# Attention ahead of a mixture of experts: work moved between VectorE, GpSimd and ScalarE, products of several query chunks in one PSUM bank, row maxima in half tiles

## The chip, the core and the metric

The kernel runs on one core of one Trainium2 chip. Its time is the device time of one execution in microseconds (us); the median of the runs is what counts. Engines: TensorE (PE, matmuls into PSUM), VectorE (DVE), ScalarE (ACT, activations), GpSimd (POOL) and SyncE (SP, which issues the DMAs here).

## What is computed

```python
q_pool = q.reshape(B, H, S // 2, 2, D).mean(axis=3)          # B, H, S, D = 4, 8, 1152, 64
scores = scale * np.matmul(q_pool, k.transpose(0, 1, 3, 2))
scores = scores - np.max(scores, axis=-1, keepdims=True)
attn = np.exp(scores)
attn = attn / (np.sum(attn, axis=-1, keepdims=True) + 1e-09)
x = np.matmul(attn, v)
```

The result x (2304 rows of 512) goes through a mixture of experts in which each of eight experts takes exactly 288 rows, picked by the largest logits (h = relu(x w1), y = h w2), and then through a feed-forward layer with g = h cos(h) between its two products. The products need more than half precision, so operands are held as a high and a low half in float16 and multiplied in three products, hi*hi, hi*lo and lo*hi.

## The kernel before

Attention is worked off in 16 units. A unit is one head of two batches, called sides 0 and 1; side 0 has queries 0 to 511 and a rest of 64, side 1 a rest of 64 and 512 more, so that a unit has nine chunks of 128 queries, of which chunk 4 holds the two rests. The keys of a side are nine blocks of 128.

For every unit:

- The operands are loaded and split (`prep_q` L342, `prep_k` L384, `prep_v` L422, the last two once for each side). `upper` (L327) writes the high half on ScalarE or GpSimd, a scalar_tensor_tensor on VectorE the low half (L372, L404, L440); DMA transposes turn q and k.
- `row_max` (L487) multiplies a chunk of queries with eight blocks of keys into a pair of PSUM banks s (two pairs in turn), and one VectorE reduction of 1024 columns (L496) takes the maximum; `last_max` (L467) does the ninth block for four chunks at a time, in banks t. `shift` (L500) joins the two maxima (L508) and writes them in two halves, 16 copies each, beside q (L511, L513), so that a matmul subtracts them from the scores.
- `piece` (L547): the scores of a unit are made with the keys on the partitions, in eleven pieces. Ten have 1024 columns in two PSUM banks t (three banks in turn), the eleventh 128. ScalarE takes exp of each bank into a float32 tile p (L565). Pieces 3 and 8 are used as they are, in float32. For the other nine ScalarE makes the high half ph (L597, one instruction of 1024 columns), and the low half pl = p - ph is divided between GpSimd (columns from d on, L607) and VectorE (columns below d, L614), with d chosen so that both would end together.
- `product` (L644): for each chunk of queries, ph and pl of all keys are multiplied with v and a column of ones into the one bank acc; `evac` (L669) adds the two parts of 65 columns on VectorE (L671).
- `finish` (L706): the sum is inverted (L713, L715), the result scaled (L339, on VectorE or GpSimd), for every second unit split into halves xs (L738 on ScalarE, L740 on VectorE), stored, turned, and multiplied with the gate weights into logits.

The order of the instructions on each engine is made when the kernel is built, by class `Order` (L72): tasks ask for an engine and a number of columns, a table COST counts the engines' time, and each task has a rank (ten to a unit). The engines then run their lists strictly in that order. Besides, `split64` (L189) splits pieces of the float64 weight w_in with what time is left: 23 of its 32 pieces come before the end of attention.

After attention, `moe` does the routing (a search by bits on VectorE and TensorE that begins with a maximum over the logits, L940), the experts and the last layer.

## Time and profile before

| | us |
|---|---|
| median of 3 runs | 1282.27 (1281.61 to 1290.19) |
| span of the profiled execution, first to last instruction | 1280.3 |
| busy in the span: PE / DVE / ACT / POOL | 1070.1 / 988.0 / 714.7 / 550.7 |
| attention: first scores to last | about 33 to 553 |

The page does not give a device time of its own for the profiled execution; the median lies 2.0 us above its span. Busy times are those in which an engine works on instructions, waits for data or a port inside an instruction included. The ends of matmuls are modelled.

### The profile page before, as it was taken

Reading aid. Unit: us, or ns where it says so; the run is one execution under the profiler, and the core shown is the slowest. Engines: PE = TensorE matmul, PEld = TensorE weight load, DVE = VectorE, ACT = ScalarE, POOL = GpSimd, SP = SyncE. Lnnn points to the kernel's source line nnn. Section 1 sums busy time; section 2 is a strip of 40 time slices with the busy share of each in tenths; the row PEclk is TensorE's granted clock in tenths of the full one; section 3 lists DMA queues with packets and bytes.
Section 4 is the critical chain, followed back from the end, with each engine's and each line's share of the span. In section 5 each row is a group of like instructions: output and inputs, shape, how many; then the busy total and the mean of one; then the engine's idle time right before and its main releaser. Section 6 shows DMA issues by size and latency. Waiting matters only on the chain. (4 is left out here: it accounts for less than half of the span.)

```text
span 1280.3 us, 26070 instructions
## 1 busy us (share of the span) xinstructions
PE 1070.1 (84%) x10281; PEld 729.8 (57%) x10281; DVE 988.0 (77%) x1927; ACT 714.7 (56%) x1324; POOL 550.7 (43%) x474
## 2 busy tenths in 40 slices
PE   3788877888788787851687999999999999999997
PEld 1355555555555555541464575766757576676763
DVE  7999999999999999779699686493847746271632
ACT  2766667677676767756577353362524436261533
POOL 1674667666666755547467112121120313030222
PEclk9999889999898989975798999999999999999999
DMA  6855655665566353234543262412223243300000
GB/s 183 208 117 140 150 124 131 141 136 139 129 128 121 81 121 63 51 96 142 153 139 100 77 170 70 117 44 77 68 101 86 75 112 85 74 29 17 1 17 17
DMA packets 195546, 128.93 MB, mean 101 GB/s; under 512 B 143008, under 2 KB 161440, under 8 KB 195424
## 3 DMA queue, kind: packets, MB, share of 16 engines
q1 hardware_dynamic: 192448, 117.83, 37.3%
q0 software_dynamic: 2976, 9.44, 2.2%
q8 instruction: 80, 1.31, 0.4%
q14 instruction: 42, 0.34, 0.1%
HBM read 83.40 MB, written 9.45 MB: 73 GB/s over the span
## 5 line engine op out<-in xcount | busy, mean ns | idle before, releaser
L607 POOL TENSOR_TENSOR pl<-p,ph 128x832 f16<-128x832 f32 (+6 forms) x128 | 222.9, 1745 | 98.2 <-ACT ph L597 74.5
L1294 POOL TENSOR_TENSOR gl<-turns,gh 128x512 f16<-128x512 f32 x72 | 89.0, 1243 | 306.8 <-ACT gh L1292 306.6
L565 ACT ACTIVATE p<-t 128x512 f32<-128x512 f32 x256 | 146.4, 593 | 103.2 <-PE t L578 84.0
L636 PE MATMUL acc<-vv,ph 128*128 128x130 f16 (+1 forms) x1124 | 129.2, 227 | 81.9 <-DVE o L671 80.1
L496 DVE TENSOR_REDUCE nm<-s 128x1 f32<-128x1024 f32 x144 | 173.9, 1211 | 1.7 <-PE s L453 1.5
L1309 PE MATMUL h<-yh,wih 128*128 128x256 f16 x576 | 158.5, 275 | 0.9 <-DVE turns L1287 0.9
L1309 PE MATMUL h<-yh,wil 128*128 128x256 f16 x576 | 157.8, 274 | 0.0
L1309 PE MATMUL h<-yl,wih 128*128 128x256 f16 x576 | 157.8, 274 | 0.0
L636 PEld LDWEIGHTS <-pl 128*128 128x128 f16 (+1 forms) x1152 | 97.1, 104 | 94.9 <-issue 88.9
L578 PE MATMUL t<-q,k 96*128 96x512 f16 (+1 forms) x576 | 143.5, 304 | 3.3 <-DMA q<-q 3.3
L577 PE MATMUL t<-q,k 128*128 128x512 f16 (+1 forms) x576 | 142.9, 304 | 3.0 <-ACT p L565 2.3
L597 ACT ACTIVATE ph<-p 128x1024 f16<-128x1024 f32 x128 | 134.8, 1054 | 1.3
L1204 DVE SCALAR_TENSOR_TENSOR hl<-h,hh 128x288 f16<-128x288 f32 x64 | 29.1, 454 | 121.2 <-ACT hh L1202 121.2
L636 PE MATMUL acc<-vv,pl 128*128 128x65 f16 (+1 forms) x1124 | 121.6, 197 | 0.4 <-DVE pl L614 0.4
L636 PEld LDWEIGHTS <-ph 128*128 128x128 f16 (+1 forms) x1152 | 107.2, 110 | 25.7 <-issue 15.3
L1309 PEld LDWEIGHTS <-wih 128*128 128x128 f16 x1152 | 108.4, 98 | 16.7 <-issue 1.2
L1335 PE MATMUL o<-woh,gl 128*128 128x512 f16 x288 | 110.3, 383 | 3.9 <-POOL gl L1294 3.9
L1335 PE MATMUL o<-wol,gh 128*128 128x512 f16 x288 | 110.3, 383 | 0.9 <-POOL wol L239 0.9
L1335 PE MATMUL o<-woh,gh 128*128 128x512 f16 x288 | 110.4, 383 | 0.1
L453 PE MATMUL s<-k,q 128*128 128x512 f16 (+1 forms) x320 | 93.9, 408 | 13.2 <-DVE nm L496 12.1
L1230 PE MATMUL h<-xx,w1h 128*128 128x288 f16 x512 | 97.5, 291 | 0.4 <-ACT xx L1116 0.4
L1335 PEld LDWEIGHTS <-gh 128*128 128x128 f16 x576 | 54.4, 98 | 66.7 <-issue 6.6
(267 smaller groups left out, 2623.9 us busy)
## 6 DMA issues: line engine op xcount, KB each, us to landing
wraw<-in_moe_w_dram SPq DMA_DIRECT2D x64, 512.0 KB, 5.0
kr<-in_k_dram SPq DMA_DIRECT2D x32, 288.0 KB, 3.1
vr<-in_v_dram SPq DMA_DIRECT2D x32, 288.0 KB, 3.0
qr<-in_q_dram SPq DMA_DIRECT2D x32, 256.0 KB, 3.5
raw<-in_moe_w_in_dram SPq DMA_DIRECT2D x32, 256.0 KB, 3.0
raw<-in_moe_w_out_dram SPq DMA_DIRECT2D x32, 256.0 KB, 3.0
k<-k SPq DMA_DIRECT2D x32, 144.0 KB, 2.8
x_dram<-xs SPq DMA_DIRECT2D x16, 160.0 KB, 2.6
```

Source lines behind the costliest of these rows:

```text
L453: T.matmul(to[lo:hi], ops["q", u][0][:, c, lo:hi], ops["k", u, i][0][:, keys, :].rearrange("p a b -> p (a b)"), start=True, stop=True)
L496: V.tensor_reduce(st["nm", u][:, c:c + 1], s, AX.XY, OP.max)
L565: A.activation(p[:, bank:bank + w], s[:, :w], AF.Exp, scale=QK_DOWN)
L577: T.matmul(s[:, to:to + w], k1[:, j], q1[:, cols], start=True, stop=False)
L578: T.matmul(s[:, to:to + w], k2[0:96, j], q2[0:96, cols], start=False, stop=True)
L597: A.activation(ph, p, AF.Copy)
L607: G.tensor_tensor(pl[:, d:], p[:, d:], ph[:, d:], op=OP.subtract)
L636: T.matmul(acc[lo:hi, a:2 * (D + 1)], t[z][:, at:at + hi - lo], vv[:, j, a:], start=j == first and z == 0, stop=j == last and z == 1, skip ...
L1230: nc.tensor.matmul(ph[:, :CAP].rearrange("p (j t) -> p j t", j=3), x[:, kk, fs], y[:, :, kk], start=kk == 0 and z == 0, stop=kk == KD - 1 ...
L1294: nc.gpsimd.tensor_tensor(gl[:, f:f + 2], g, gh[:, f:f + 2], op=OP.subtract)
L1309: nc.tensor.matmul(u[:, e * NB:(e + 1) * NB], x[:, kk, fs], y[:, kk], start=kk == 0 and z == 0, stop=kk == KD - 1 and z == 2)
L1335: nc.tensor.matmul(po, x[:, f, cs], y[:, f], start=f == 0 and z == 0, stop=f == NF2 - 1 and z == 2)
```

## The change

- Two pieces of the ten, 1 and 6 (`CP`), get their halves another way: ScalarE takes exp of the PSUM bank twice, once into ph in float16 and once in place, and VectorE subtracts ph from the bank into pl. For six other pieces and the small one, GpSimd makes all of pl, each bank of 512 columns by itself (exp, copy, subtract). p becomes six tiles of 512 columns.
- A row maximum is two reductions of 512 columns in single banks s (three in turn, which `last_max` now uses too, instead of t); a reduction of three columns a row joins them.
- The multiplications in `shift`, the sum with 1e-9, the scaling of x and the low half of xs go to GpSimd, as does the sum of the query pairs. `upper` on GpSimd is a tensor_scalar with a number instead of a tensor_tensor with a broadcast column, and counts half in the planner's choice.
- k and v of both sides are split in one instruction of 1152 columns instead of two of 576 (k of unit 0 apart); v has one buffer for both sides.
- `product` takes groups of chunks, (0, 1), (2, 3), (5, 6) and (7, 8, 4), side by side in one bank acc (two in turn); neighbours are added by one reduction of 260 columns. Banks: t 3, s 4, acc 1 before; t 3, s 3, acc 2 after.

```diff
+CP = 1, 6
...
-            e = yield [(ACT, n), (POOL, n)]
+            e = yield [(ACT, n), (POOL, n // 2)]
             if e == ACT:
-                A.activation(out, src, AF.Copy, scale=256.0 if by is up else 128.0)
+                A.activation(out, src, AF.Copy, scale=by)
             else:
-                G.tensor_tensor(out, src, wide(by, list(src.shape)), op=OP.mult)
...
-            yield from either(qs, r[:, :, 0:D], r[:, :, D:], OP.add)
+            yield POOL, HC * D
+            G.tensor_tensor(qs, r[:, :, 0:D], r[:, :, D:], op=OP.add)
...
+            r = raw.tile([128, 2, KJ, D], F32, name="vr", bufs=1)
...
+            V.scalar_tensor_tensor(t[:, :, :, 0, 0:D], r, 256.0, t[:, :, :, 1, 0:D], op0=OP.mult, op1=OP.subtract)
...
-            slot = yield from turn("t", 3)
+            slot = yield from turn("s", 3)
...
-            slot = yield from turn("s", 2)
-            s = ps.tile([128, 2, 512], F32, name="s", bufs=2)
-            yield PE, 1024 if len(sides(c)) < 2 else 1120
             for g in range(2):
-                products(s[:, g], u, c, slice(4 * g, 4 * g + 4))
-            yield DVE, 1024
-            V.tensor_reduce(st["nm", u][:, c:c + 1], s, AX.XY, OP.max)
+                slot = yield from turn("s", 3)
+                s = ps.tile([128, 512], F32, name="s", bufs=3)
+                yield PE, 512 if len(sides(c)) < 2 else 560
+                products(s, u, c, slice(4 * g, 4 * g + 4))
+                start(largest(u, c, g, s, slot), 10 * u - RK[2] + c)
+        def largest(u, c, g, s, slot):
+            yield DVE, 512
+            V.tensor_reduce(st["nm", u][:, c, g:g + 1], s, AX.X, OP.max)
             mark(*slot)
-            mark("nm", u, c)
+            mark("nm", u, c, g)
...
-            t2, nm, n = q2s[u % 2], st["nm", u][:, c0:c1], c1 - c0
-            yield DVE, n
-            V.tensor_tensor(nm, nm, st["lm", u][:, c0:c1], op=OP.max)
-            src = nm.unsqueeze(2).to_broadcast([128, n, 16])
-            yield DVE, 16 * n
-            V.tensor_tensor(t2[:, c0:c1, 64:80], src, wide(down, [128, n, 16]), op=OP.mult)
-            yield DVE, 16 * n
-            V.scalar_tensor_tensor(t2[:, c0:c1, 80:96], src, QK_DOWN, t2[:, c0:c1, 64:80], op0=OP.mult, op1=OP.subtract)
+            t2, n = q2s[u % 2], c1 - c0
+            yield DVE, 3 * n
+            nm = opd.tile([128, 2, n], F32, name=f"mx{n}", bufs=2)
+            V.tensor_reduce(nm[:, 0], st["nm", u][:, c0:c1], AX.X, OP.max)
+            yield POOL, 24 * n
+            G.tensor_scalar(t2[:, c0:c1, 64:80], nm[:, 0].unsqueeze(2).to_broadcast([128, n, 16]), QK_DOWN, None, op0=OP.mult)
+            G.tensor_scalar(nm[:, 1], nm[:, 0], QK_DOWN, None, op0=OP.mult)
+            yield POOL, 16 * n
+            G.tensor_tensor(t2[:, c0:c1, 80:96], nm[:, 1].unsqueeze(2).to_broadcast([128, n, 16]), t2[:, c0:c1, 64:80], op=OP.subtract)
...
             def exp(s, bank, w, bslot):
+                b = slice(bank, bank + w)
+                if not whole and not near:
+                    slot = yield from turn("p", 6)
+                    f = pp.tile([128, 512], F32, name="p", bufs=6)
                 yield ACT, w
-                A.activation(p[:, bank:bank + w], s[:, :w], AF.Exp, scale=QK_DOWN)
-                mark(*bslot)
-                mark("exp", u, x, bank)
+                if whole:
+                    A.activation(p[:, b], s[:, :w], AF.Exp, scale=QK_DOWN)
+                    mark(*bslot)
+                elif near:
+                    A.activation(ph[:, b], s[:, :w], AF.Exp, scale=QK_DOWN)
+                    yield ACT, w
+                    A.activation(s[:, :w], s[:, :w], AF.Exp, scale=QK_DOWN)
+                    yield DVE, w
+                    V.tensor_tensor(pl[:, b], s[:, :w], ph[:, b], op=OP.subtract)
+                    mark(*bslot)
+                else:
+                    A.activation(f[:, :w], s[:, :w], AF.Exp, scale=QK_DOWN)
+                    mark(*bslot)
+                    yield ACT, w
+                    A.activation(ph[:, b], f[:, :w], AF.Copy)
+                    yield POOL, w
+                    G.tensor_tensor(pl[:, b], f[:, :w], ph[:, b], op=OP.subtract)
+                    mark(*slot)
...
-            d = (b - a - LAG + COST[POOL][1] * n) / (COST[DVE][1] + COST[POOL][1])
-            d = 32 * round(min(max(d, LO * n), HI * n) / 32)
-            od.free[POOL] += COST[POOL][1] * (n - d)
-            G.tensor_tensor(pl[:, d:], p[:, d:], ph[:, d:], op=OP.subtract)
...
-                    V.tensor_tensor(pl[:, :d], p[:, :d], ph[:, :d], op=OP.subtract)
...
-            slot = yield from turn("acc", 1)
-            acc = ps.tile([128, 512], F32, name="acc", bufs=1)
-            yield PE, sum(290 if c == 4 else 515 if st["p", u, sides(c)[0][2], j, main(sides(c)[0][2]).start][1] is None else 204 for j in range(KJ))
-            pv(acc, u, c, range(KJ))
-            st["left", u] = st.get(("left", u), HC) - 1
-            for x in range(NP):
-                if c in users(x):
-                    n = st["left", u, x] = st.get(("left", u, x), len(users(x))) - 1
...
+            slot = yield from turn("acc", 2)
+            acc = ps.tile([128, 512], F32, name="acc", bufs=2)
+            for n, c in enumerate(cs):
+                yield PE, sum(290 if c == 4 else 515 if st["p", u, sides(c)[0][2], j, main(sides(c)[0][2]).start][1] is None else 204 for j in range(KJ))
+                pv(acc, u, c, range(KJ), to=n * 2 * (D + 1))
...
-                yield DVE, 130
-                V.tensor_reduce(st["o", u][:, c], acc[:, :2 * (D + 1)].rearrange("p (s d) -> p d s", s=2), AX.X, OP.add)
+                yield DVE, 130 * len(cs)
+                at = 0
+                while at < len(cs):
+                    n = 1
+                    while at + n < len(cs) and cs[at + n] == cs[at] + n:
+                        n += 1
+                    V.tensor_reduce(st["o", u][:, cs[at]:cs[at] + n],
+                                    acc[:, 2 * (D + 1) * at:2 * (D + 1) * (at + n)].rearrange("p (c s d) -> p c d s", c=n, s=2), AX.X, OP.add)
+                    at += n
...
-            V.tensor_tensor(r[:, 0], o[:, c0:c1, D], tiny.to_broadcast([128, n]), op=OP.add)
+            G.tensor_scalar(r[:, 0], o[:, c0:c1, D], 256.0 * 1e-9, 1.0 / X_UP, op0=OP.add, op1=OP.mult)
...
-            yield from either(x[:, c0:c1, (h % 2) * D:(h % 2 + 1) * D], o[:, c0:c1, :D],
-                              r[:, 1].unsqueeze(2).to_broadcast([128, n, D]), OP.mult)
+            yield POOL, n * D
+            G.tensor_tensor(x[:, c0:c1, (h % 2) * D:(h % 2 + 1) * D], o[:, c0:c1, :D],
+                            r[:, 1].unsqueeze(2).to_broadcast([128, n, D]), op=OP.mult)
...
-            yield DVE, 128 * n
-            V.scalar_tensor_tensor(xs[:, c0:c1, 1], x[:, c0:c1], X_UP, xs[:, c0:c1, 0], op0=OP.mult, op1=OP.subtract)
+            A.activation(xs[:, c0:c1, 0], x[:, c0:c1], AF.Copy)
+            yield POOL, 128 * n
...
```

The planner makes other lists from this. On VectorE, a piece of unit 5 before (s is a pair of banks with the products for the maxima, nm their maxima, pl the low half of p, ks the halves of k):

```order
L496 TENSOR_REDUCE nm<-s 128x1
L614 TENSOR_TENSOR pl<-p,ph 128x224
L508 TENSOR_TENSOR nm<-nm,lm 128x5
L671 TENSOR_REDUCE o<-acc 128x65
L511 TENSOR_TENSOR q_122<-nm,down 128x5x16
L513 SCALAR_TENSOR_TENSOR q_122<-nm,q_122 128x5x16
L404 SCALAR_TENSOR_TENSOR ks<-kr,ks 128x9x64
L496 TENSOR_REDUCE nm<-s 128x1
L671 TENSOR_REDUCE o<-acc 128x65
L614 TENSOR_TENSOR pl<-p,ph 128x256
L404 SCALAR_TENSOR_TENSOR ks<-kr,ks 128x9x64
L496 TENSOR_REDUCE nm<-s 128x1
```

and the like place of a unit in the changed kernel (mx joins the maxima; t is a bank of scores; line numbers are those of the changed kernel):

```order
L481 TENSOR_REDUCE nm<-s 128x1 x2
L496 TENSOR_REDUCE mx_4025<-nm 128x5
L481 TENSOR_REDUCE nm<-s 128x1 x2
L388 SCALAR_TENSOR_TENSOR ks<-kr,ks 128x18x64
L660 TENSOR_REDUCE o<-acc 128x130
L481 TENSOR_REDUCE nm<-s 128x1 x3
L425 SCALAR_TENSOR_TENSOR vv_108<-vr,vv_108 128x18x64
L481 TENSOR_REDUCE nm<-s 128x1
L574 TENSOR_TENSOR pl<-t,ph 128x512 x2
L660 TENSOR_REDUCE o<-acc 128x130
```

L614, L511 and L513 are gone from VectorE; what is left with both inputs in SBUF are the low halves of the operands.

On GpSimd, ten rows of a middle unit before (vv are the halves of v, mag and low those of w_in):

```order
L607 TENSOR_TENSOR pl<-p,ph 128x800
L607 TENSOR_TENSOR pl<-p,ph 128x640
L333 TENSOR_TENSOR vv_118<-vr,up 128x9x64
L607 TENSOR_TENSOR pl<-p,ph 128x832
L333 TENSOR_TENSOR vf_121<-vr,up 128x2x64
L231 TENSOR_TENSOR mag<-mag,low 128x256
L607 TENSOR_TENSOR pl<-p,ph 128x672
L607 TENSOR_TENSOR pl<-p,ph 128x832
L235 TENSOR_TENSOR low<-low,sg 128x256
L239 TENSOR_TENSOR wil<-low,wih 128x256
```

and of a middle unit in the changed kernel:

```order
L716 TENSOR_TENSOR x<-o,r_3868 128x4x64
L582 TENSOR_TENSOR pl<-p,ph 128x512
L498 TENSOR_SCALAR q_112<-mx_4025 128x5x16
L499 TENSOR_SCALAR mx_4025<-mx_4025 128x5
L582 TENSOR_TENSOR pl<-p,ph 128x512
L501 TENSOR_TENSOR q_112<-mx_4025,q_112 128x5x16
L582 TENSOR_TENSOR pl<-p,ph 128x512
L319 TENSOR_SCALAR vv_108<-vr 128x18x64
L582 TENSOR_TENSOR pl<-p,ph 128x512 x3
L705 TENSOR_SCALAR r_4195<-o 128x5
L582 TENSOR_TENSOR pl<-p,ph 128x512
L498 TENSOR_SCALAR q_112<-mx_4225 128x4x16
```

The steps of `shift` (L498, L499, L501) and of `finish` (L705, L716) now stand in GpSimd's list among the subtractions L582. Over the whole of attention VectorE has 30 of the sums and subtractions of `split64` (18 before) and GpSimd 16 (28 before); 23 pieces of w_in begin before its end in both.

## Rows read from the trace of the kernel before

**Rows 1.** Busy time of VectorE in tenths, in 40 slices of the span.

```profile
DVE  7999999999999999779699686493847746271632
```

**Rows 2.** Busy time by engine from 33 to 553 us: PE, PEld, DVE, ACT, POOL, granted clock.

```profile
33.00:553.00 520.00, 416.20 (x4601) 278.68 (x4600) 497.85 (x779) 367.44 (x637) 339.25 (x257) 0.94 0.55 121
```

**Rows 3.** VectorE by line, 33 to 553 us: count, busy us, mean ns, idle before.

```profile
L496 DVE TENSOR_REDUCE nm<-s 128x1 f32<-128x1024 f32 x135 | 163.3, 1211 | 1.5 <-PE s L453 1.3
L614 DVE TENSOR_TENSOR pl<-p,ph 128x192 f16<-128x192 f32 (+6 forms) x127 | 87.5, 690 | 2.0 <-ACT ph L597 2.0
L440 DVE SCALAR_TENSOR_TENSOR vv<-vr,vv 128x576 f16<-128x576 f32 x32 | 41.6, 1303 | 0.1
L671 DVE TENSOR_REDUCE o<-acc 128x65 f32<-128x130 f32 x139 | 39.1, 282 | 14.6 <-PE acc L636 14.5
L404 DVE SCALAR_TENSOR_TENSOR ks<-kr,ks 128x576 f16<-128x576 f32 x28 | 27.6, 987 | 0.0
...
L508 DVE TENSOR_TENSOR nm<-nm,lm 128x5 f32<-128x5 f32 (+1 forms) x30 | 20.1, 672 | 0.0
L513 DVE SCALAR_TENSOR_TENSOR q<-nm,q 128x80 f16<-128x80 f32 (+1 forms) x30 | 18.3, 611 | 0.1
L339 DVE TENSOR_TENSOR x<-o,r 128x320 f32<-128x320 f32 (+1 forms) x23 | 16.6, 722 | 0.3
L511 DVE TENSOR_TENSOR q<-nm,down 128x80 f16<-128x80 f32 (+1 forms) x30 | 15.7, 523 | 0.0
L713 DVE TENSOR_TENSOR r<-o,tiny 128x4 f32<-128x4 f32 (+1 forms) x30 | 14.3, 476 | 0.4
...
L740 DVE SCALAR_TENSOR_TENSOR xs<-x,xs 128x512 f16<-128x512 f32 (+1 forms) x14 | 11.4, 816 | 0.1
...
L789 DVE TENSOR_TENSOR logits<-logits,t 128x32 f32<-128x32 f32 (+1 forms) x10 | 1.8, 178 | 0.4 <-PE t L781 0.4
```

**Rows 4.** VectorE in order of time, around 205 and 219 us: start, duration, instruction.

```profile
205.24 1.10 DVE L508 TENSOR_TENSOR nm<-nm,lm 128x5 f32<-128x5 f32 x1
206.26 0.28 DVE L671 TENSOR_REDUCE o<-acc 128x65 f32<-128x130 f32 x1
...
218.85 0.75 DVE L440 SCALAR_TENSOR_TENSOR vv<-vr,vv 128x576 f16<-128x576 f32 x1
```

**Rows 5.** GpSimd in order of time, around 205, 215 to 219 and 229 us.

```profile
205.03 1.29 POOL L333 TENSOR_TENSOR ks<-kr,up 128x576 f16<-128x576 f32 x1
...
215.36 1.75 POOL L607 TENSOR_TENSOR pl<-p,ph 128x832 f16<-128x832 f32 x1
...
218.87 2.04 POOL L607 TENSOR_TENSOR pl<-p,ph 128x672 f16<-128x672 f32 x1 [0.28 <-ACT ph L597]
...
228.93 1.46 POOL L607 TENSOR_TENSOR pl<-p,ph 128x672 f16<-128x672 f32 x1 [1.00 <-ACT ph L597]
```

**Rows 6.** VectorE by form, 60 to 480 us: a reduction of 512 columns from PSUM.

```profile
L481 DVE TENSOR_REDUCE lm<-t 128x4 f32<-128x512 f32 x25 | 16.9, 677 | 0.4 <-PE t L453 0.3
```

**Rows 7.** ScalarE by line, 33 to 553 us.

```profile
L565 ACT ACTIVATE p<-t 128x512 f32<-128x512 f32 x253 | 144.6, 593 | 96.1 <-PE t L578 76.8 <-issue 17.3
L597 ACT ACTIVATE ph<-p 128x1024 f16<-128x1024 f32 x128 | 134.8, 1054 | 1.3
```

**Rows 8.** GpSimd's iotas, which read no tensor, by form.

```profile
L165 POOL IOTA jp<- 128x128 f32 x1 | 0.2, 245 | 0.4 <-POOLq L1368 0.4
...
L853 POOL IOTA w<- 128x8 f32 x1 | 0.1, 138 | 2.0 <-DVE r L715 2.0
```

**Rows 9.** Waits from 60 to 480 us: us in total, times, longest.

```profile
PE acc L636 <- DVE o L671: 68.5, 52, 3.6
...
POOL x L339 <- DVE r L715: 10.1, 4, 3.5
```

**Rows 10.** VectorE, start of the routing after attention.

```profile
564.99 0.25 DVE L940 TENSOR_REDUCE m<-logits 128x18 f32<-128x144 f32 x1
```

More of the change, by code (lines that the diff above doesn't have):

```diff
@@ L547, in piece @@
         def piece(u, x, before):
-            parts, small, whole = PIECES[x], x == NP - 1, x in FP
+            parts, small, whole, near = PIECES[x], x == NP - 1, x in FP, x in CP
             n = max(col + (c1.stop - c1.start) for _, _, c1, col in parts)
@@ L582, in piece, with pv @@
                 mark("scored", u)
-            for bank in range(0, n, 512):
-                yield "exp", u, x, bank
-            if whole:
-                for i, j, cols, at in parts:
-                    st["p", u, i, j, cols.start] = p, None, at
-                st["free", u, x] = slot
-                mark("p", u, x, 0)
-                mark("p", u, x, 1)
-                return
-            hname, hbufs = ("phs", 2) if small else ("ph", PB)
-            hslot = yield from turn(hname, hbufs)
-            ph, pl = (pp.tile([128, n], F16, name=m + ("s" if small else ""), bufs=hbufs) for m in ("ph", "pl"))
-            st["free", u, x] = hslot
-            yield ACT, n
-            A.activation(ph, p, AF.Copy)
-            for i, j, cols, at in parts:
-                st["p", u, i, j, cols.start] = ph, pl, at
-            since = od.now
-            yield POOL, 0
-            a, b = (max(since, od.free[e]) + COST[e][0] for e in (DVE, POOL))
-            d = (b - a - LAG + COST[POOL][1] * n) / (COST[DVE][1] + COST[POOL][1])
-            d = 32 * round(min(max(d, LO * n), HI * n) / 32)
-            od.free[POOL] += COST[POOL][1] * (n - d)
-            G.tensor_tensor(pl[:, d:], p[:, d:], ph[:, d:], op=OP.subtract)
-            od.now = od.free[POOL] + COST[POOL][2]
-            mark("p", u, x, 0)
-            def lower():
-                if d:
-                    yield DVE, d
-                    V.tensor_tensor(pl[:, :d], p[:, :d], ph[:, :d], op=OP.subtract)
-                else:
-                    yield DVE, -60
-                mark("p", u, x, 1)
-                mark(*slot)
-            start(lower(), 10 * u + x + RK[8], since)
-        def pv(acc, u, c, js, first=0, last=KJ - 1):
+        def pv(acc, u, c, js, first=0, last=KJ - 1, to=0):
             for j in js:
@@ L635, in pv @@
                         a = (0, D + 1)[z]
-                        T.matmul(acc[lo:hi, a:2 * (D + 1)], t[z][:, at:at + hi - lo], vv[:, j, a:],
-                                 start=j == first and z == 0, stop=j == last and z == 1, skip_group_check=True)
+                        T.matmul(acc[lo:hi, to + a:to + 2 * (D + 1)], t[z][:, at:at + hi - lo], vv[:, j, a:],
+                                 start=j == first and z == 0 and to == 0, stop=j == last and z == 1, skip_group_check=True)
         def where(c, j):
@@ L799, in attention @@
             start(prep_q(u), early + 10 * u - RK[0])
-            for i in range(2):
-                start(prep_k(u, i), early + 10 * u - RK[0] + 3 + i)
-            for i in range(2):
-                start(prep_v(u, i), 10 * u - RK[1] + i)
+            for at in ((0, 1),) if u else ((0,), (1,)):
+                start(prep_k(u, at), early + 10 * u - RK[0] + 3 + at[0])
+            start(prep_v(u), 10 * u - RK[1])
             for c in range(HC):
@@ L813, in attention @@
                 before = u, x
-            for c in range(HC):
-                if u < NU - 1 or c < 4:
-                    start(product(u, c), 10 * u + (c if u == NU - 1 else RK[3] + c if c < 4 else RK[4] + c if c > 4 else RK[4] + RK[5]))
+            for cs in GROUPS:
+                if u < NU - 1 or max(cs) < 4:
+                    start(product(u, cs), 10 * u + (cs[0] if u == NU - 1 else RK[3] + cs[0] if cs[0] < 4 else RK[4] + cs[-1]))
             if u < NU - 1:
```

216 lines of the change are left out of this document (108 added, 108 removed).

## Prediction

> **What bounds the kernel now.** I read the busy shares by slice first: VectorE is at nine tenths in nearly every slice of attention, the first 18 of 40 [rows 1]. The view by windows makes that a number: from 33 to 553 us VectorE is busy for 497.9 of 520 us, 96%, and PE for 416, ScalarE for 367, GpSimd for 339 [rows 2]. Sixteen units in 520 us are 32.5 us each. The view of VectorE by line shows that it idles for almost nothing but the banks acc [rows 3]; so attention lasts as long as VectorE's list.
>
> That list is not all work. The order of time shows why: a sum of 5 columns took 1.10 us and ended at 206.34, while a GpSimd instruction ran from 205.03 to 206.32; the reduction from PSUM behind it took its normal 0.28 [rows 4, 5]. The other way, GpSimd's 672 columns took 2.04 us when they started at 218.87 just behind a VectorE instruction with two SBUF inputs (218.85, 0.75 us), and 1.46 undisturbed [rows 4, 5]. So a VectorE instruction that reads two operands in SBUF and a GpSimd instruction shut each other out, whole. VectorE with one operand in PSUM does not wait (logits plus PSUM: mean 178 ns) [rows 3]. I call the time in which either holds this "the port".
>
> **VectorE after the change.** Each instruction covers some 0.08 us of the one behind it (205.24 + 1.10 against 206.26 [rows 4]), which I take off every mean.
>
> - Gone [rows 3]: L614, 127 x 0.61 = 77 us; the three steps of the shift, 30 x (0.672 + 0.523 + 0.611 - 0.24) = 47; sum, scaling and low half of x, 30 x 0.40 + 23 x 0.64 + 14 x 0.74 = 37. Together 161.
> - Maxima: a reduction of 512 costs 677 ns [rows 6], so 270 x 0.60 = 161 us instead of 135 x 1.13 = 153: +8.
> - Pieces 1 and 6: 64 subtractions of 512 from PSUM. None is in the trace; as the reduction of 512 they cost 0.60 each, 38 us; waiting for the port as L614 did (0.69 for some 294 columns) about 0.9, 57 us. I take 38, since the logits row with the same kinds of operands does not wait.
> - Banks acc: a reduction of 260 columns lies between 282 ns for 130 and 677 for 512, 0.42 by the line; 62 of these and 15 of 130 cost 24 us instead of 28: -4.
> - Low halves of k and v: half the instructions, twice the columns. Unblocked 0.75 us for 576 [rows 4], so 1.34 for 1152; with the mean wait of today (0.55 for v, 0.24 for k, from [rows 3]) 50 us instead of 64: -14.
> - Joining maxima, 32 x 0.1 = 3; twelve more instructions of split64 by the order, 5.
>
> Sum: 498 - 161 + 8 + 38 - 4 - 14 + 8 = 373 us, 23.3 a unit. VectorE stops being the bound.
>
> **ScalarE and PE.** 128 copies of 1024 columns (135 us) become 192 of 512 and 64 second exps. A copy of 512 costs between half of 1054 ns and the 593 of an exp [rows 7]; at 0.59 for both 151 us: +16. That makes 383 us, 24.0 a unit. PE's products are the same, 416 us or 26.0 a unit at a granted clock of 0.94 [rows 2]; its wait of 68.5 us for VectorE to empty acc [rows 9] should mostly go with the second bank.
>
> **GpSimd and the port.** Undisturbed, 672 columns take 1.46 us and 832 take 1.75 [rows 5]: 0.24 us and 1.81 ns a column, 1.17 us for 512.
>
> - pl: 192 x 1.17 + 16 x 0.47 = 232 us.
> - Sums of q, 576 columns each: 16 x 1.28 = 21.
> - Operands' high halves as tensor_scalar: by the order 31 instructions with 24,192 columns. This form is not in the trace. At the rate of the two-input form (1.29 us for 576 [rows 5]) they cost 54 us; at that of an iota, which reads nothing (138 ns for 8 columns, 245 for 128 [rows 8], so 0.13 us and 0.9 ns a column), 26. I take 40, the middle, as it reads one input.
> - Shift: 64 instructions of 64 or 80 columns and 32 of 4 or 5, between 0.15 and 0.38 each: 24. Sums and scaling of x: 33 x 0.16 + 33 x 0.75 = 30. Low halves xs: 15 x 1.28 + 2 x 0.7 = 21. split64: 39 x 0.70 = 27.
>
> GpSimd alone: 395 us. VectorE's instructions with two SBUF inputs hold the port for 16 x 1.28 (v), 15 x 1.28 + 1.4 (k), 16 x 0.68 (q) and 53 x 0.34 (split64): 70 us. Together the port is taken for 465 us, 29.1 a unit.
>
> The Trainium skill, in GPSIMD Engine Reference, section 4.1 Engine selection, calls a one-input operation on GpSimd roughly line-rate. At its 1.2 GHz, 24,192 columns would be an estimated 20 us; the sum by it would be 445 us, 27.8 a unit.
>
> The same count on the kernel before: GpSimd 201 (pl) + 6 (the small pieces) + 18 (sums of q) + 46 (high halves) + 35 (split64) + 5 (x) = 311, VectorE 50 (pl) + 54 (k, v, q) + 34 (shift, x) + 14 = 152, together 463 us, 89% of 520. **The port is asked for as much as before.** What changes is who waits: before, VectorE, which had other work as well, stood behind it; now GpSimd is the engine with the longest list, and it only waits for instructions that hold the port. I expect the pair to run at the 96% that the bounding engine reaches today: 465 / 0.96 = 484 us instead of 520, 30.3 a unit.
>
> **Ends.** In the first unit the maxima cost 18 x 0.60 against 9 x 1.13, +0.6 us, and the shift goes over two engines: +1 in all. In the last, x is scaled and split on GpSimd (0.47 and 0.7 against 0.28 and 0.42 by VectorE undisturbed): +1.5. The routing, which began at 564.99 [rows 10], should begin near 531. Behind that nothing is changed, and as many pieces of w_in are split before it.
>
> Sum: -36 + 2.5 = -33.5 us against the profiled 1280.3, to which 2.0 is added for the median: 1282.3 - 33.5 = 1248.8, say 1249.
>
> **Rivals.**
>
> - The port yields more. If tensor_scalar runs near the iota's rate and GpSimd's fixed 0.24 us lies beside VectorE's turn, the port asks for 27 a unit; ScalarE and PE (24 to 26) are then equal partners: 27.5 a unit, 440 us, 1282 - 80 + 2.5 = 1205. For it speaks that VectorE's waiters start about 0.1 us before GpSimd's record ends; against it, that three engines, each about 90% busy, would hardly ever have to wait for one another. Chance 0.2.
> - No gain. Two-input rate for tensor_scalar (+14 us) and 93% instead of 96% give (465 + 14) / 0.93 = 515 us: 1282 - 5 + 2.5 = 1280. For it speaks the equal demand for the port. Chance 0.15.
> - Slower: GpSimd's list stands still for VectorE. It now waits in order for two reciprocals and two joined maxima a unit. Before, four scalings of x waited for the reciprocal for 10.1 us, 2.5 each [rows 9]; at that price four waits are 10 us a unit. Today's 32.5 is passed once they cost 32.5 - 29.1 = 3.4, or 0.85 each; at half the price, 29.1 + 5 = 34.1 a unit, 546 us: 1282 + 26 + 2.5 = 1311. Against it: the order puts one to five other instructions between a step on VectorE and the one on GpSimd that needs it, and GpSimd was early then because it had a third of its time free. The Trainium skill speaks for it: the section named above sends elementwise work to VectorE, GpSimd being about twice as slow with two inputs; the trace agrees for undisturbed instructions, 1.28 us against 0.75 for 576 columns. Chance 0.12.
>
> **How the numbers follow.** Forecast 0.53, with 1225 to 1268 as its own range; the rivals 0.2, 0.15 and 0.12. A measurement tells some 1% (13 us) from no change. Faster by over 1%, below 1269: 0.53 + 0.2, nearly: 0.72. Within 1%: 0.15. Slower: 0.13. The range reaches to the first rival and to just over no gain: 1207 to 1286.
>
> **What would show it.** Right: routing begins at 525 to 540; from 33 us to the last scores VectorE is busy for about 75 to 80%, GpSimd above 85%; L574 takes about 0.68 us with no wait in it, L582 1.2 to 1.3 on average, the tensor_scalar of 1152 columns 1.2 to 2.6. Wrong: GpSimd idle before x or the shift for more than 3 us a unit; L574 near 1 us; ScalarE or PE above 95%; a stretch after attention that lasts longer than 715 us.

## The result, and the profile after

| | before | after |
|---|---|---|
| median, us | 1284.18 (1281.61 to 1290.19) | 1225.78 (1225.07 to 1229.83) |
| ratio | | 0.9547 [0.9514, 0.9581] |
| span of the profiled execution | 1280.3 | 1223.5 |
| first exp / last exp of attention | 30.4 / 554.1 | 37.7 / 500.3 |
| routing begins (maximum over the logits) | 564.99 [rows 10] | 511.01 |
| from there to the end | 715.3 | 712.5 |

The change makes the kernel faster by 4.5%, 58 us, where 33.5 were forecast; the time lies inside the range, at the low end of the forecast's own 1225 to 1268. All but 3 us of it comes from attention: the 16 units take 463 us from first to last exp instead of 524, 28.9 us each instead of 32.7, and the first exp comes 7 us later. As before, 23 pieces of w_in are begun ahead of the routing.

The page of the changed kernel, busy time in tenths in 40 slices (compare [rows 1]):

```profile
DVE  6888677989788985597996774846838473461632
...
POOL 4889899999999988566673041130312204030212
```

The nines have gone from VectorE to GpSimd. By windows, 33 to 495 us of the changed kernel (us, busy time and count of PE, PEld, DVE, ACT, POOL, then granted clock, DMA share, GB/s):

```profile
33.00:495.00 462.00, 409.76 (x4609) 274.35 (x4608) 371.06 (x632) 361.50 (x734) 427.92 (x454) 0.96 0.60 135
```

GpSimd is busy for 93% of this stretch, PE for 89, VectorE for 80 and ScalarE for 78. Against [rows 2] VectorE has lost its 96%, and the others have all moved closer to the bound. GpSimd by line, from the start to the routing (count, busy us, mean ns, idle before and what ended it):

```profile
L582 POOL TENSOR_TENSOR pl<-p,ph 128x512 f16<-128x512 f32 x192 | 240.8, 1266 | 9.9 <-ACT ph L580 8.8
L319 POOL TENSOR_SCALAR vv<-vr 128x1152 f16<-128x1152 f32 x11 | 35.2, 3204 | 0.9 <-PE acc L617 0.7
L340 POOL TENSOR_TENSOR qs<-qr 128x576 f32<-128x576 f32 x16 | 22.7, 1417 | 9.4 <-DMA qr<-in_q_dram 6.1 <-DVE q L353 3.2
L716 POOL TENSOR_TENSOR x<-o,r 128x320 f32<-128x320 f32 (+2 forms) x33 | 22.5, 682 | 2.4 <-DVE r L707 2.0 <-PE t L597 0.3
L733 POOL TENSOR_TENSOR xs<-x,xs 128x640 f16<-128x640 f32 (+2 forms) x17 | 20.8, 1224 | 0.1
...
L319 POOL TENSOR_SCALAR ks<-kr 128x1152 f16<-128x1152 f32 x5 | 15.7, 3142 | 9.8 <-DMA kr<-in_k_dram 7.8 <-issue 1.6 <-DMA k<-ks 0.4
L498 POOL TENSOR_SCALAR q<-mx 128x80 f16<-128x80 f32 (+1 forms) x32 | 15.6, 486 | 10.0 <-DVE mx L496 9.8
...
L501 POOL TENSOR_TENSOR q<-mx,q 128x80 f16<-128x80 f32 (+1 forms) x32 | 10.3, 322 | 0.6
L319 POOL TENSOR_SCALAR qq<-qs 128x576 f16<-128x576 f32 x6 | 9.9, 1653 | 0.4
...
L319 POOL TENSOR_SCALAR vf<-vr 128x256 f32<-128x256 f32 x9 | 8.8, 972 | 0.2
L499 POOL TENSOR_SCALAR mx<-mx 128x5 f32<-128x5 f32 (+1 forms) x32 | 8.4, 262 | 0.0
```

Two things are to be seen. The idle time before x and the shift is small: 2.4 and 10.6 us in 16 units. And the four rows of L319, `upper` as a tensor_scalar, come to 69.6 us. VectorE by line, the same stretch (compare [rows 3]):

```profile
L481 DVE TENSOR_REDUCE nm<-s 128x1 f32<-128x512 f32 x288 | 187.3, 679 | 13.6 <-PE s L439 12.6
L574 DVE TENSOR_TENSOR pl<-t,ph 128x512 f16<-128x512 f32 x64 | 41.1, 676 | 8.5 <-ACT t L572 8.5
L425 DVE SCALAR_TENSOR_TENSOR vv<-vr,vv 128x1152 f16<-128x1152 f32 x16 | 32.6, 2037 | 15.5 <-POOL vv L319 15.5
L660 DVE TENSOR_REDUCE o<-acc 128x130 f32<-128x260 f32 (+1 forms) x77 | 29.0, 393 | 12.7 <-PE acc L617 12.7
L388 DVE SCALAR_TENSOR_TENSOR ks<-kr,ks 128x1152 f16<-128x1152 f32 (+1 forms) x17 | 26.4, 1555 | 21.4 <-POOL ks L319 10.7 <-ACT ks L317 8.0 <-DMA qr<-in_q_dram 2.4
```

The new subtraction L574 takes 676 ns, just as long as a reduction of 512 columns from PSUM, 679: a VectorE instruction with one operand in PSUM does not wait for GpSimd (all 64 took between 653 and 693 ns). The low halves L425 and L388, with both inputs in SBUF, do, and they also stand behind GpSimd's slow high halves. How the two engines meet is seen in the order of time, GpSimd first (start, duration, instruction):

```profile
207.54 3.15 POOL L319 TENSOR_SCALAR vv<-vr 128x1152 f16<-128x1152 f32 x1
210.66 4.50 POOL L582 TENSOR_TENSOR pl<-p,ph 128x512 f16<-128x512 f32 x3
...
216.15 1.16 POOL L582 TENSOR_TENSOR pl<-p,ph 128x512 f16<-128x512 f32 x1
217.26 0.91 POOL L716 TENSOR_TENSOR x<-o,r 128x320 f32<-128x320 f32 x1
```

and VectorE in the same stretch (the idle time before an instruction, and what ended it, in brackets):

```profile
204.51 1.36 DVE L388 SCALAR_TENSOR_TENSOR ks<-kr,ks 128x1152 f16<-128x1152 f32 x1 [0.88 <-ACT ks L317]
...
210.72 2.31 DVE L425 SCALAR_TENSOR_TENSOR vv<-vr,vv 128x1152 f16<-128x1152 f32 x1 [2.02 <-POOL vv L319]
...
216.37 1.21 DVE L223 SCALAR_TENSOR_TENSOR mag<-raw,down 128x256 int32<-128x256 int32 x1
```

L425 needs 1.36 us undisturbed (as L388 shows) and took 2.31; three L582 beside it took 4.50 us instead of 3 x 1.16 = 3.48. GpSimd thus lost 1.0 us to an instruction of 1.36 us. The VectorE instruction of 216.37 lost 0.8 us itself (the median of L223 is 0.42 us). GpSimd's subtraction that ran beside it lost nothing, but the scaling of x behind it (L716) took 0.91 us, the longest of all, where its form of 320 columns takes 0.78 on the mean.

### The profile page after: what moved, and what is told of

The parts are those of the page before. It is cut to its first block, busy times and chain, and to the rows that moved or that the text cites. A ratio compares the mean times of both kernels' runs of the same rounds, so it can differ in the third digit from the quotient of the medians.

```text
span 1223.5 us, 26093 instructions
## 1 busy us (share of the span) xinstructions
PE 1064.9 (87%) x10281; PEld 724.9 (59%) x10281; DVE 854.0 (70%) x1759; ACT 705.8 (58%) x1417; POOL 660.1 (54%) x687
## 5 line engine op out<-in xcount | busy, mean ns | idle before, releaser
L582 POOL TENSOR_TENSOR pl<-p,ph 128x512 f16<-128x512 f32 x192 | 240.8, 1266 | 9.9 <-ACT ph L580 8.8
L481 DVE TENSOR_REDUCE nm<-s 128x1 f32<-128x512 f32 x288 | 187.3, 679 | 13.6 <-PE s L439 12.6
L439 PE MATMUL s<-k,q 128*128 128x512 f16 (+3 forms) x480 | 129.4, 351 | 45.6 <-DVE nm L481 26.9
L596 PE MATMUL t<-q,k 128*128 128x512 f16 (+1 forms) x576 | 138.4, 295 | 26.8 <-ACT p L577 11.1
L597 PE MATMUL t<-q,k 96*128 96x512 f16 (+1 forms) x576 | 138.4, 296 | 0.7 <-DMA q<-q 0.7
L577 ACT ACTIVATE p<-t 128x512 f32<-128x512 f32 (+1 forms) x208 | 115.9, 577 | 39.0 <-PE t L597 36.3
L617 PE MATMUL acc<-vv,ph 128*128 128x130 f16 (+1 forms) x1124 | 124.8, 226 | 0.0
L580 ACT ACTIVATE ph<-p 128x512 f16<-128x512 f32 x192 | 117.3, 636 | 0.4
L617 PE MATMUL acc<-vv,pl 128*128 128x65 f16 (+1 forms) x1124 | 117.5, 196 | 0.0
```

Source lines behind the costliest of these rows:

```text
L439: T.matmul(to[lo:hi], ops["q", u][0][:, c, lo:hi], ops["k", u, i][0][:, keys, :].rearrange("p a b -> p (a b)"), start=True, stop=True)
L481: V.tensor_reduce(st["nm", u][:, c, g:g + 1], s, AX.X, OP.max)
L577: A.activation(f[:, :w], s[:, :w], AF.Exp, scale=QK_DOWN)
L580: A.activation(ph[:, b], f[:, :w], AF.Copy)
L582: G.tensor_tensor(pl[:, b], f[:, :w], ph[:, b], op=OP.subtract)
L596: T.matmul(s[:, to:to + w], k1[:, j], q1[:, cols], start=True, stop=False)
```

## The experiments

All are edits of the changed kernel. Differences in us against it are differences of the two ratios times 1284, the time of the kernel before; an interval of a ratio of +-0.004 is 5 us, and a difference of two such ratios is good to 5 to 8 us. In the expectations A says that GpSimd's own list sets the time, B that GpSimd's list and the port do, C that PE and ScalarE do; D says that all engines work in order with some slack each, so that a us on any of them has a price. In the runs that double work, the work is done twice with the same result.

**Other numbers of near pieces.** Two runs change the table CP, and with it what the planner makes.

```diff
-CP = 1, 6
+CP = ()
```

> The changed kernel with no piece subtracted from PSUM: pieces 1 and 6 go the way of the others, 64 more subtractions of 512 columns on GpSimd (1.27 us each in the changed kernel, 81 us), 64 fewer on VectorE (0.60, 38 us), as many ScalarE instructions. Theory A (GpSimd's own list is the bound, 94% busy from 100 to 450 us): the kernel grows by most of 81 us, to some 1295 to 1305. Theory B (the port, all that either engine holds of it): the same sum, 1295 to 1305. Theory C (PE and ScalarE, 89% and 78% busy from 33 to 495 us): within 10 us of 1226.

Measured: 1242.01 us, ratio 0.9661 [0.9608, 0.9714], 15 us slower than the changed kernel. The sum hides two movements. Routing began at 492.07 us, 19 us *earlier*, but only 6 pieces of w_in had been begun by then instead of 23, and the stretch behind it took 748.5 us instead of 712.5. GpSimd was busy for 345.6 of 350 us from 100 to 450, and the planner had given the high halves of v to ScalarE (1 on GpSimd instead of 11). None of the theories' numbers came (75 us slower, or within 10). So this is no undoing of one part: the planner answered it with other lists.

```diff
-CP = 1, 6
+CP = 1, 4, 6
```

> The changed kernel with a third piece, 4, subtracted from PSUM by VectorE: 32 subtractions of 1.27 us (41 us) leave GpSimd, 32 of 0.60 (19 us) come to VectorE. Theories A and B: about 30 to 38 us faster than 1226, 1188 to 1196, as long as VectorE (371 us busy of 462) and the three banks t don't take over. Theory C: within 8 us of 1226. If the banks t bind, which this piece holds through two exps and a subtraction: slower than 1226.

Measured: 1233.16 us, 0.9587 [0.9537, 0.9638], some 5 us slower, at the edge of what the runs tell apart; routing at 524.68 with 27 pieces begun, PE's wait for L574 to empty a bank t 18.7 us instead of 8.8. It tells no theory from another for the same reason. In the next six runs and in the undoing of pieces 1 and 6 the tasks' requests to the planner were left as they are, and only what they issue was changed; the last three runs change the requests again.

**VectorE with two operands in SBUF, more of it.** The low halves of k and v twice:

```diff
             V.scalar_tensor_tensor(t[:, b, :, D:], r[:, b], 256.0, t[:, b, :, 0:D], op0=OP.mult, op1=OP.subtract)
+            V.scalar_tensor_tensor(t[:, b, :, D:], r[:, b], 256.0, t[:, b, :, 0:D], op0=OP.mult, op1=OP.subtract)
...
             V.scalar_tensor_tensor(t[:, :, :, 0, 0:D], r, 256.0, t[:, :, :, 1, 0:D], op0=OP.mult, op1=OP.subtract)
+            V.scalar_tensor_tensor(t[:, :, :, 0, 0:D], r, 256.0, t[:, :, :, 1, 0:D], op0=OP.mult, op1=OP.subtract)
```

> The changed kernel with the low halves of k and v each computed twice into the same place: 33 more VectorE instructions with two inputs in SBUF, 1.27 us each undisturbed, 41 us. Theory A: GpSimd loses only what it lost to such instructions so far (some 30 us in place of the 70 that they hold the port, 0.4 of their length), about 16 us: 1236 to 1246. Theory B: the port is held 41 us longer and the kernel grows by nearly all of it: 1262 to 1270. Theory C: within 5 us of 1226.

Measured: 1277.91 us, 0.9932 [0.9907, 0.9957], 49 us slower; routing at 562.09, 51 later. The added rows of VectorE by line:

```profile
L427 DVE SCALAR_TENSOR_TENSOR vv<-vr,vv 128x1152 f16<-128x1152 f32 x16 | 31.9, 1993 | 0.6
...
L389 DVE SCALAR_TENSOR_TENSOR ks<-kr,ks 128x1152 f16<-128x1152 f32 (+1 forms) x17 | 32.2, 1895 | 0.6
```

Undisturbed these are about 41 us, and they cost 49, or 1.2 us a us, with VectorE busy for only 86% from 100 to 450 us. A, which said 10 to 20, falls: GpSimd's own list is what it was. B's 36 to 44 come close. GpSimd's instructions, the same as before, lasted longer: up to the routing it was busy for 480.9 us in place of 451.7, most of it in the subtractions (240.8 us in the changed kernel):

```profile
L584 POOL TENSOR_TENSOR pl<-p,ph 128x512 f16<-128x512 f32 x192 | 259.1, 1361 | 14.5 <-ACT ph L582 13.6
```

**VectorE from PSUM, more of it.** 64 of the reductions of 512 columns twice:

```diff
             V.tensor_reduce(st["nm", u][:, c, g:g + 1], s, AX.X, OP.max)
+            if c in (1, 3, 6, 8) and g == 0:
+                V.tensor_reduce(st["nm", u][:, c, g:g + 1], s, AX.X, OP.max)
```

> Beside the run with the low halves twice: 64 reductions of 512 columns from PSUM done twice, 38 us more for VectorE with no operand read from SBUF. Theories A, B and C: VectorE is at 80%, so 0 to 8 us over 1226. A rival, that VectorE's list is still what counts: 25 to 38 us over, 1251 to 1264.

Measured: 1242.07 us, 0.966 [0.961, 0.971], 14 us slower for the following row; 64 x 0.60 = 38 us on VectorE, so 0.38 us a us. Routing at 527.92, 17 later.

```profile
L483 DVE TENSOR_REDUCE nm<-s 128x1 f32<-128x512 f32 x64 | 44.3, 692 | 2.2
```

That is more than the 8 that A, B and C allow at most and less than the 25 of the rival, VectorE's list. A us of VectorE from PSUM costs a third of one with two operands in SBUF. The difference, 0.8, is put down to the port, and the rows of GpSimd bear it out: here it was busy up to the routing for 451.9 us, as in the changed kernel, with the low halves twice for 29 more.

```profile
L584 POOL TENSOR_TENSOR pl<-p,ph 128x512 f16<-128x512 f32 x192 | 237.0, 1246 | 10.9 <-ACT ph L582 9.6
```

**GpSimd, less of it.** `upper` in the form of before, with two inputs, in the same places:

```diff
-                G.tensor_scalar(out, src, by, None, op0=OP.mult)
+                G.tensor_tensor(out, src, wide(cols[by], list(src.shape)), op=OP.mult)
```

> The changed kernel with the operands' high halves on GpSimd in the old two-input form (a tensor_tensor with a broadcast column in place of tensor_scalar), every engine's order kept. In the changed kernel tensor_scalar took 3.2 us for 1152 columns, 69.6 us in all; the two-input form cost 1.29 for 576 before, some 2.4 for 1152, 52 us in all: 17 us less for GpSimd. Theory A (GpSimd's own list is the bound): 14 to 17 us faster than 1226, 1209 to 1212. Theory B (the port): the same. Theory D (all engines in order, each with some slack; only VectorE's two-input instructions count in full): 5 to 9 us faster, 1217 to 1221.

Measured: 1211.85 us, 0.9433 [0.9396, 0.947], 15 us *faster* than the changed kernel, routing at 497.26. GpSimd by line:

```profile
L328 POOL TENSOR_TENSOR vv<-vr,up 128x1152 f16<-128x1152 f32 x11 | 23.7, 2158 | 1.1 <-PE acc L626 0.7 <-DMA vr<-in_v_dram 0.4
```

2.16 us instead of 3.20 for the same columns; over the four tiles 48.1 us instead of 69.6. The multiplication with a second input is the cheaper form, and 21.5 us less on GpSimd give 0.68 us a us. A and B said 14 to 17, D 5 to 9; 15, good to some 6, speaks for the former without ruling out D.

**GpSimd, more of it.** The scaling of x and the low half of xs twice:

```diff
+            G.tensor_tensor(x[:, c0:c1, (h % 2) * D:(h % 2 + 1) * D], o[:, c0:c1, :D],
+                            r[:, 1].unsqueeze(2).to_broadcast([128, n, D]), op=OP.mult)
...
+            G.tensor_tensor(xs[:, c0:c1, 1], x[:, c0:c1], xs[:, c0:c1, 0], op=OP.subtract)
```

> The changed kernel with the scaling of x and the low half of xs done twice on GpSimd into the same place, order kept: 43 us more for GpSimd, with SBUF operands. Theories A and B: 38 to 45 us slower, 1264 to 1271. Theory D: about half, as for VectorE's maxima (38 us more cost some 16): 15 to 25 us slower, 1241 to 1251.

Measured: 1260.1 us, 0.9813 [0.9789, 0.9837], 34 us slower for 43 us of instructions (22.5 + 20.8 by the rows of the changed kernel), 0.79 us a us; routing 37 later. That lies between A and B (38 to 45) and D (15 to 25).

**ScalarE, more of it.** The first exp of the near pieces twice:

```diff
                     A.activation(ph[:, b], s[:, :w], AF.Exp, scale=QK_DOWN)
+                    A.activation(ph[:, b], s[:, :w], AF.Exp, scale=QK_DOWN)
```

> The changed kernel with the first exp of pieces 1 and 6 done twice into the same place, order kept: 64 ScalarE instructions of 0.61 us, 35 us more for ScalarE, which is 78% busy. Theories A and B: 0 to 6 us slower. Theory D: 10 to 20 us slower, 1236 to 1246.

Measured: 1237.44 us, 0.9644 [0.962, 0.9668], 12 us slower for 35 us, 0.36 us a us; routing 9 later. That is D's range; A and B allowed 6. ScalarE isn't the bound, as a us of GpSimd costs twice as much, but it isn't free either.

**Undoing: shift and x back on VectorE.** Emission alone; the tasks still ask for GpSimd, so the lists keep their order as far as that goes.

```diff
-            G.tensor_scalar(t2[:, c0:c1, 64:80], nm[:, 0].unsqueeze(2).to_broadcast([128, n, 16]), QK_DOWN, None, op0=OP.mult)
+            V.tensor_scalar(t2[:, c0:c1, 64:80], nm[:, 0].unsqueeze(2).to_broadcast([128, n, 16]), QK_DOWN, None, op0=OP.mult)
...
-            G.tensor_tensor(xs[:, c0:c1, 1], x[:, c0:c1], xs[:, c0:c1, 0], op=OP.subtract)
+            V.tensor_tensor(xs[:, c0:c1, 1], x[:, c0:c1], xs[:, c0:c1, 0], op=OP.subtract)
```

(and the other two steps of the shift, the sum and the scaling of x in the same way)

> The changed kernel with the shift rows and the sum, scaling and low half of x given back to VectorE, order kept as far as it goes: some 87 us leave GpSimd, VectorE gets 177 instructions with SBUF operands that stood for 84 us before the change. Theory A: GpSimd's list shrinks by a fifth, 40 us or more faster, below 1190. Theory B: the port is asked for some 45 us less, 30 to 45 us faster, 1181 to 1196. Theory D: VectorE pays about 80 us with a share of 0.4 to 1.2 and GpSimd gains about half of 87: between 10 us faster and 40 us slower, 1216 to 1266.

Measured: 1255.85 us, 0.9792 [0.9761, 0.9823], 31 us slower; routing at 539.09. By windows, 100 to 450 us of this run:

```profile
100.00:450.00 350.00, 299.64 (x3353) 200.51 (x3353) 322.14 (x586) 260.56 (x521) 256.41 (x199) 0.94 0.61 135
```

GpSimd has fallen to 73% and VectorE risen to 92%. The numbers of A and B, a kernel faster by 30 us and more, did not come; but both left VectorE's list out, and with VectorE at 92% this run alone doesn't refute them for the changed kernel. D's range has the result. VectorE is made the busiest engine again. Its smallest instructions show the price: the scaling of five joined maxima takes 0.41 us on it, against 0.26 on GpSimd:

```profile
L499 DVE TENSOR_SCALAR mx<-mx 128x5 f32<-128x5 f32 (+1 forms) x32 | 13.2, 412 | 0.0
```

**Undoing: pieces 1 and 6 on GpSimd**, with the order and the planner's choices of the changed kernel:

```diff
-                    A.activation(ph[:, b], s[:, :w], AF.Exp, scale=QK_DOWN)
+                    f2 = pp.tile([128, 512], F32, name="p", bufs=6)
+                    A.activation(f2[:, :w], s[:, :w], AF.Exp, scale=QK_DOWN)
...
-                    A.activation(s[:, :w], s[:, :w], AF.Exp, scale=QK_DOWN)
+                    A.activation(ph[:, b], f2[:, :w], AF.Copy)
...
-                    V.tensor_tensor(pl[:, b], s[:, :w], ph[:, b], op=OP.subtract)
+                    G.tensor_tensor(pl[:, b], f2[:, :w], ph[:, b], op=OP.subtract)
```

> The changed kernel with pieces 1 and 6 split as the other pieces (exp into SBUF, copy, subtraction on GpSimd) but every engine's order and every operand choice kept, which the run without near pieces did not: 64 more subtractions of 1.27 us on GpSimd (81 us), 64 fewer on VectorE (38 us), ScalarE the same. By what the runs so far gave for a us more (about 0.85 for GpSimd, 0.4 for VectorE): 69 - 15 = 54 us slower, about 1280, no better than the kernel before. Theory A and B: 75 to 81 us slower, above 1300. If this part bought little, as the run without near pieces seemed to say: within 20 us of 1226.

Measured: 1286.53 us, 1.0007 [0.9987, 1.0027], 59 us slower, near the 54 of the prices and short of the 75 to 81 of A and B: with these lists there is no gain at all without this part. Routing at 569.33. By windows and GpSimd's added row by line:

```profile
100.00:450.00 350.00, 290.51 (x3107) 191.39 (x3105) 236.24 (x384) 242.94 (x488) 340.75 (x346) 0.90 0.57 126
```

```profile
L575 POOL TENSOR_TENSOR pl<-p,ph 128x512 f16<-128x512 f32 x64 | 76.2, 1199 | 0.1
```

GpSimd is at 97%, VectorE at 67%. This is the mirror of [rows 2].

**Undoing: one chunk in a bank**, still with two banks acc:

```diff
-GROUPS = (0, 1), (2, 3), (5, 6), (7, 8, 4)
+GROUPS = (0,), (1,), (2,), (3,), (5,), (6,), (7,), (8,), (4,)
```

> The changed kernel with one chunk of queries to a bank acc, as before, but with two banks in turn: 144 reductions of 130 columns in place of 77 (62 of them of 260), 5 us more for VectorE. All theories: 0 to 5 us slower, 1226 to 1231. If it is the sharing of a bank that made PE's wait for acc go, more: PE waits again, 10 us or more slower.

Measured: 1227.58 us, 0.9547 [0.9509, 0.9584], the same. PE's wait for VectorE to empty acc comes back with 10.8 us between 100 and 450 us, where the changed kernel lists none and the kernel before had 62.2; so most of that wait went with the second bank, and the rest with the sharing. That sharing is worth nothing is not shown, though: the groups are requests to the planner, and its lists changed (high halves of v on GpSimd 7 in place of 11, of k 7 in place of 5; 22 pieces of w_in begun; routing at 506.47, 5 us earlier, and 719.6 us behind it).

**High halves away from GpSimd.** First all of `upper` on ScalarE:

```diff
-            e = yield [(ACT, n), (POOL, n // 2)]
-            if e == ACT:
-                A.activation(out, src, AF.Copy, scale=by)
-            else:
-                G.tensor_scalar(out, src, by, None, op0=OP.mult)
+            yield ACT, n
+            A.activation(out, src, AF.Copy, scale=by)
```

> The changed kernel with all high halves of the operands on ScalarE, known to the planner: 69 us of tensor_scalar leave GpSimd, about 26 us come to ScalarE (1.1 to 1.2 us for 1152 columns). By 0.7 to 0.85 for a us on GpSimd and 0.3 to 0.36 on ScalarE: 49 to 59 us less and 8 to 9 more, 40 to 50 us faster than 1226, 1176 to 1186. Rival: PE and ScalarE take over as soon as GpSimd is at 80%: 10 to 25 us faster, 1200 to 1216.

Measured: 1194.91 us, 0.9294 [0.9257, 0.9331], 32 us faster than the changed kernel, routing at 474.73. It lies between what was expected (40 to 50) and the rival (10 to 25); from 100 to 450 us GpSimd is at 87% here, PE at 94% and ScalarE at 90%. Then `upper` wholly as it was before, form and price for the planner (with the run's two-input form from above):

```diff
-            e = yield [(ACT, n), (POOL, n // 2)]
+            e = yield [(ACT, n), (POOL, n)]
...
-                G.tensor_scalar(out, src, by, None, op0=OP.mult)
+                G.tensor_tensor(out, src, wide(cols[by], list(src.shape)), op=OP.mult)
```

> The changed kernel with one part undone whole: the operands' high halves on GpSimd in the two-input form and at their full count in the planner's choice, as before the change; the planner then gives GpSimd two of q and ten of vf in place of 31, and ScalarE the rest. GpSimd: some 10 us of such work instead of 69, ScalarE some 20 us more than in the changed kernel. By 0.65 to 0.85 for a us on GpSimd and 0.26 to 0.36 on ScalarE: 38 to 50 us less and 5 to 7 more, so 31 to 45 us faster than 1226, 1181 to 1195; by the run with all on ScalarE, which fell short of such a sum: 1192 to 1202. If this part of the change was a gain: slower than 1226.

Measured: 1190.88 us, 0.9256 [0.9223, 0.9289], 37 us faster than the changed kernel and the best of all runs; routing at 469.20, with 22 pieces of w_in begun and 717.4 us behind it. The planner made new lists in both of these runs, so that the 37 are those of the form and of the planner's choice together; the form alone, with the lists held, gave 15. By windows, the changed kernel and then this one:

```profile
100.00:450.00 350.00, 315.03 (x3622) 214.14 (x3621) 289.82 (x499) 277.31 (x561) 329.28 (x350) 0.96 0.64 139
```

```profile
100.00:450.00 350.00, 328.19 (x3967) 224.43 (x3966) 282.70 (x515) 311.21 (x627) 319.68 (x373) 1.00 0.67 141
```

In the same 350 us it does 10% more matmuls (3967 against 3622); GpSimd is at 91%, ScalarE at 89% and PE at 94%, at a granted clock of 1.00, the 2.4 GHz level, where the changed kernel has a mean of 0.96. All high halves of v are now written by ScalarE, for 1.19 us each instead of 3.20 on GpSimd:

```profile
L326 ACT ACTIVATE vv<-vr 128x1152 f16<-128x1152 f32 x16 | 19.0, 1188 | 0.8 <-DMA vr<-in_v_dram 0.8
```

## Why the prediction was right, and where its size was off

The prediction named faster with 0.72, VectorE's list as the bound before, GpSimd with the port as the bound after, and the routing as the place where the gain shows. The trace agrees with each of these, with the third only in part: GpSimd is the busiest engine, but the runs give a us on each of four engines a price. Point by point:

- *"VectorE stops being the bound", 373 us.* Busy 371 us from 33 to 495, 80%. The "wrong" sign, L574 near 1 us, did not come: 0.676 us, 0.60 of it by the prediction's way of counting, the lower of the two bounds.
- *Rival "GpSimd's list stands still for VectorE"* did not happen. x and the shift waited for 11.8 us in all for VectorE's joined maxima and reciprocals (9.8 and 2.0 by the rows), 0.7 us a unit, against the 3.4 a unit from which it decides; the other instructions in between covered the steps, as the order had it.
- *ScalarE 383, PE 416.* Neither is above 90%; PE's wait for VectorE to empty acc [rows 9] is gone from the longest waits. Two more of the predicted signs held: the stretch after attention, 712.5 us, and L582, 1.27 us on the mean. Two missed: the routing began at 511 and not between 525 and 540, and the tensor_scalar of 1152 columns took 3.2 us and not 1.2 to 2.6.
- *"GpSimd alone: 395 us", "70 us" for the port, together 465.* GpSimd's rows up to the routing add up to 461 us, waits inside an instruction included. The sum is right by two errors that cancel. Its own work was dearer by about 40: the high halves as tensor_scalar took 69.6 us, above the 54 that were the upper bound and far from the 40 taken, and the shift 34 instead of 24. The port cost it less: 192 L582 at 1.266 instead of 1.16 are 20 us of waiting, with the rest of its list perhaps 27, not 70. That is no fixed share: the low halves done a second time cost GpSimd 29 us for 41. The reason shows in the order of time above: GpSimd loses less than VectorE's instruction lasts (1.0 of 1.36 us), and little (0.1 us in the rows above) where VectorE is the one that waits. So the first rival was right that the port yields more, and wrong on tensor_scalar.
- *The Trainium skill*, GPSIMD Engine Reference, section 4.1 Engine selection, with its one-input operation at roughly line rate, does not hold for this form: the estimate from it was 20 us for the same columns, the trace has 69.6, 3.2 us for 1152 columns, and the two-input form is the faster one, 2.16 (48.1 us in all, less than the 54 that the prediction gave it). For two inputs the prediction had 1.28 us against VectorE's 0.75 for 576 columns, from its sum of rows; undisturbed they took 1.15 in the run with two inputs, 1.5 times VectorE's time.
- *"465 / 0.96 = 484 us", 30.3 a unit.* This is the step of the forecast that was mis-sized: measured were 463, 28.9 a unit, and attention lost 61 us where 36 were named. The whole of GpSimd's list, as a sum of rows, was put against the 16 units. But rows of neighbours overlap a little (207.54 + 3.15 against 210.66 above); the prediction took that off for VectorE and not for GpSimd, whose 461 us by rows are 452 by windows. Of these 15 lie before 33 us (high halves and sums of the first units) and 8 behind 495. In between it was busy for 428 us of 462. The other half of the step, 96% for the pair, was too high, 93%, and hid part of this.
- *"Ends: +2.5".* From last exp to routing it took 10.8 us (10.9 before), but the first exp came 7.2 us later, which took 5 us back. VectorE in order of time shows where:

```profile
25.48 1.36 DVE L388 SCALAR_TENSOR_TENSOR ks<-kr,ks 128x1152 f16<-128x1152 f32 x1 [2.36 <-DMA qr<-in_q_dram]
26.75 5.26 DVE L481 TENSOR_REDUCE nm<-s 128x1 f32<-128x512 f32 x8
```

  and GpSimd beside it:

```profile
22.32 3.12 POOL L319 TENSOR_SCALAR ks<-kr 128x1152 f16<-128x1152 f32 x1 [7.83 <-DMA kr<-in_k_dram]
...
32.30 1.48 POOL L498 TENSOR_SCALAR q<-mx 128x80 f16<-128x80 f32 x1 [2.48 <-DVE mx L496]
```

  VectorE's list has the low half of a later k ahead of eight maxima of the first unit. It stood still for 2.4 us until GpSimd had written the high half (the row names a DMA as the releaser, but the high half ended at 25.44, where VectorE began), and GpSimd had begun it late and took 3.12 us. The prediction named no such wait in the first unit. The slow form is a part of it: with two inputs the first exp came at 36.05, 1.6 us earlier. What made the rest, the merged k or other changes in the lists, no run takes apart. Routing: -61 + 7.2 = -54, where -33.5 were named; another 3 us came behind it.

Where did the 58 us come from? From the runs that keep the order, a us of GpSimd costs 0.7 to 0.8 us, a us of VectorE from PSUM 0.38, one of ScalarE 0.36, and one of VectorE with two operands in SBUF 1.2, about the sum of the first two, since it stops both. By the intervals 0.79 and 1.2 are good to some 0.13, 0.36 and 0.38 to 0.2, 0.68 to 0.3. That is more than a single bound: four engines work off fixed lists, are 79 to 94% busy from 100 to 450 us, and wait for one another. The parts, each undone by itself, are worth 59 us (pieces 1 and 6 to VectorE from PSUM), 31 (shift and x to GpSimd), 0 (shared banks) and -37 (`upper`). The first two are prices at these lists: when the planner could answer, leaving pieces 1 and 6 to GpSimd cost 15 and not 59; the last two hold the planner's answer. They don't add up to 58, and need not, since an undoing can make another engine the one that counts. The price of 0.8 for GpSimd would give only about 46 us for the 76.2 us of the pieces less the VectorE time saved (0.8 x 76 - 0.38 x 38); the 59 measured are more, with GpSimd at 97% there, where hardly anything may cover a us any more; that is argued and not tested.

The equal count for the port, 465 us to 463 before, was the argument for the rival "No gain". It added both engines' instructions as if the two could only take turns; with losses inside the instructions of some 27 us where 70 were counted, it is no such sum.

Not tried by themselves: the maxima in half tiles, the merging of k's and v's instructions, and the third buffer that goes from s to acc. Open too is what part of the clock plays: from 100 to 450 us the granted clock is 0.93 in the kernel before (PE busy for 81%), 0.90 with pieces 1 and 6 undone (83%), 0.96 in the changed kernel (90%) and 1.00 with `upper` undone (94%). Whether a clock nearer 2.4 GHz is a cause or only the mark of fewer waits no run here tells apart.
